# Strassen block sums and one convolution tap moved from VectorE to ScalarE copies and GpSimd's adding DMAs, with a third pair and a new instruction order

## The chip, the cores and the metric

The kernel runs on one core of one Trainium2 chip. The metric is the device time of one execution in microseconds (us). Five engines work beside each other, each through its own instructions in order: TensorE (PE: matrix products into PSUM), VectorE (DVE), ScalarE (ACT), GpSimd (POOL) and SyncE (SP), which here only issues DMAs. An instruction waits for semaphores that other engines or DMAs raise; whatever stands behind it on its engine waits too.

## The reference

Eight batches of 576 tokens go through a packed attention in eight heads and then a gated layer. All is float32.

```python
p_packed = sm_attn(p, k, v)              # 32 packed queries a head attend to k, v
out = sm_attn(q, p_packed, p_packed)     # q attends to the 32 packed rows
x = out.transpose(0, 2, 1, 3).reshape(B, S, H * D)           # [8, 576, 512]
h = np.maximum(x @ w_in, 0.0)                                # [8, 576, 1024]
conv_out = sum(conv_w[k] * hp[:, k:k+S, :] for k in range(3))  # hp: h padded by a zero row at both ends
gate = 1.0 / (1.0 + np.exp(-conv_out))
return h * gate @ w_out                                      # [8, 576, 512]
```

## The kernel before

**Precision.** Every large product is made of three: each operand is split into a rounded high part (hi, made by an ACT copy that rounds) and the rest (lo, a DVE subtraction), and hi·hi, lo·hi and hi·lo are added in PSUM.

**Stages of a batch.** Two groups of four heads a batch (16 groups g) go through `attention`. `packed_weight` folds the packed rows into w_in, and its result is split into `ghi` and `glo`. `ffn1(b, j)` makes 128 of the 1024 hidden columns of batch b (j from 0 to 7): 12 row groups of L705 on PE, then on ACT the relu into one of three `hbuf` buffers (L717) and the middle tap into `hgt` (L721), on DVE the two outer taps (L723, L727), on ACT the tanh (L731) and on DVE the gate (L733). `hgt` has two buffers, for even and odd batches.

**Last product.** The 4608 tokens form 36 tiles of 128 (m). A plain tile takes 24 matmuls of 128x512 columns (L794); its operand is split by ACT and DVE first (L744 and L747, or in two blocks by L850 and L853). Its result is copied by ACT (L858) and stored by SP (L860).

**Pairs.** Two tiles m and m+1 with m in `PAIRS = (29, 32)` are multiplied together by Strassen's scheme in Winograd's form: each is cut into two column blocks (A11, A12 of tile m and A21, A22 of tile m+1), w_out into four quarters, and seven products P of 12 matmuls of 128x256 columns (L926, `products`) stand in for 48 of 128x512. The price is sums: four of token blocks, S1 to S4, a pair (`combined`, one DVE instruction each, L894; S2 needs S1, S4 needs S2), four of weights, T1 to T4, once (`whole_quarter` L966 and `weight_sum` L978, two DVE instructions each), a split of each (L897 and L899; L989 and L991), and two additions a pair in `results` (L951).

**Order.** `ORDER`, a string of two-character numbers, says whose step comes next; there is a stream of steps for each load, group, weight, `ffn1`, tile and sum. `Flow.run` takes them in that order, checks each against a small model of the engines, and emits them; every engine then runs its instructions as they were emitted. The model's constants (`ISSUE`, `LATER`, `SLACK`) alter the emitted program in one way only: where the model sees PE wait before the first tile of the last product, `fill` puts in dummy products of the identity (L251, "idle" in the rows).

**Start.** Loads are issued by SP in order. Up to eight of them fly at once. PE's first product of a later stage is the `packed_weight` of batch 0 (L641), which waits for the loads of groups 0 and 1; its `ghi` and `glo` are needed by the first `ffn1`, and those of its second half by `ffn1(0, 4)`.

Of the kernel before, what the change touches and what calls it, by code (L numbers as in the profile page):

```python
# [26 lines left out]
    "1a0u1n0m0u124f6e1n451l4d4e4f6e0u454f4d1a4h1c4e4e0u0u4f4g1b0y1k4d451b4i4f4f114j4i881n884k4i6e1g4h6f4j6e6e4i6f6e4k"
    "4h4k4i4j4i89161i121a4k4j4i6e1i6f6f121e1a4j4k4l891d126f6f6f6f4j4k4l1i6f1o4k6g121s4l1i4l6g4h124l8a4m1a4l6f1a1j4m1q"
    "191j1i1a6f4m4j121i6g1q8a1w6g6h6e4n6g4m6h1q204n1a1v6g1i6g4m1v4l1h6g4m1a4n124m121r1v4n6g6g236f8b1a6g4o121i4n1i4o4p"
    "6h6h4o4p4p1a236h124o8b4o6h4n1q6g4p1a6h6h6h4p6h4o1m4o1a1y4n234p4p1q1i6h1i1q4q282b1y4r6i1r1y6i1y1a1i6i126i6i1q1a2b"  # L30
    "4r6i12241a4q4q1z6i6j1a6i1a4r1i6i6i4s6i2b1p4s6j4s1q4t4u1q4s1i1y1i4t4s264t1t4t1q1z6k1y2g6j2c4u6j1y4u4s261i6j2j4u6j"
    "4s6k6j264u2j4v4t2j1q6j271i4u1u4v226i4u6j266j4t2e1x4w2k6j4t1i4v1q2e1i1q6k4w2e4v2a1i1q6h2f2e4v3p6k6k6k4w1y1i274x26"
    "6k1q6k6l1y4x6l216k6k6k2f4x1q6k4x2m1y4v50266m1q6l6l4w264v1q26262r2m6l2h4w6l2m2r506l4x2r6j6l4y4w2e1q2n2z4y4y2z1y1y"
    "2z374x1q296l2n2o6l6l6l4w4z4z1y1y4y4z516m4y6m6m6m6m6m1q4y6m6m504z4x4z514z4y524z256n6m526n536m52536n526n1y52535452"
    "536n54546n6n6n6n6n1y1y522w552m2e6o54556o1y266n2s51532u2e2u6n5a54376o6p5553556p1y552654546o3c305a1y6o6o6o6o372e2e"
    "6o6o2p1y6o265656566p6p266p6p532u556q6m26562u576p5556266p6p57566p3f576q56586p59266q6q576q6q58582d5957592m58583457"
    "58596q6q6q596o6q575859596r2e26322m5a6q6r26262e6s5b6r6r6r3226262m2e326s2m2m6r2i6p5b6r2e5c6r6r6q5b6r5c322e5d335c6r"
    "3f3f6s5c6s2v5c2u2e5c2v2e2e2e6s5e6t5c6t355f385d5d5d5d6s6s6s6s2l5f5f5e5e2e6s3a5e5d3a2m6s2m2u2m5k3a5f2m5d2u2q3b2u6t"
    "6u6u6t6r6t6t5f5e5k5f2m5g5f5e6t6t6t5k6t3g6t5h6u6u6u326u5h5h2t6s2m2m6u3a6v5h2m5h5e5h6u6u2x332u6u2m2e5h2y2e5i5j5g5g"
    "6t5i5g2m5i3i5j6v325i5j6u5l3i2u325l325i5j5j3b5g2u362m5i5i2m6v6v6v6v3a2u5j3i5g5j2u5g6v326v6v6v6v6v6w5m5m5l6w313i2u"  # L40
    "2u6x6x5n5n5o6w6w6w6w2u6w2u5n6w6w5o5m6u5m5o6w6w323j3a5m5o5o5n6x6x2u6x6x6y326x6x5n5o5o5m5n3i5m3a3a6x5n5p5p5q5p325q"
    "6x5r3d6y3e396x325p5p5q5q2u5q5p6y6y323a325p5r5r6y6y6y6y6y2u5s2u5q5q5t6y6z6x3j32325r5u325s6w32323a5t6z5r325t3i5s5t"
    "6y5r5v5s5t5s3i6z5s6z3i5r5s6z6z6z6z6z6z5t5u6y5t5u70706z3a3a5w5w703a707071828470705x5w3h5v715w5x70708070705y71715w"
    "83813a3a70715y5w855y5x5x7172835w5y725y5x713i717185715v715z5z72725z5z723a3a723i5z3a5z713i64725x73645y5z727272603i"
    "723i7386605x3i607473733a73723i6z615y607g60643i3i3a60607373733a6162747362627373636174637474747473623i636261636274"
    "3i6563613i63633i656162816175747466676587747466757j7h686666676766757575676867836675767575756766686775757j696a7k7k"
# [1022 lines left out]
```

## Time and profile before

| | |
|---|---|
| median of 3 runs | 403.42 us (401.45 to 403.48) |
| profiled execution, its own time | 402.01 us |
| its span, first to last instruction | 400.2 us |
| PE busy | 392.2 us (98%) |
| DVE busy | 365.5 us (91%) |
| ACT busy | 284.1 us (71%) |
| POOL busy | 1.6 us |
| granted TensorE clock | 0.999 |

1.8 us of the profiled execution lie outside its span. An engine's busy time is the time in which an instruction of it runs. Matmuls are pipelined and their ends are modelled, so how fast PE works is read from the distance between starts, as the chain of waits gives it, and a DVE or ACT instruction's cost to its successor is likewise start to start, some 0.1 us below its duration.

### The profile page before, as it was taken

How to read it: one execution, taken by the hardware profiler on the slowest of the kernel's cores; microseconds unless marked ns; L12 is line 12 of the kernel's file. 1: busy time of each engine (PE TensorE's matmuls, PEld its weight loads, DVE VectorE, ACT ScalarE, POOL GpSimd, SP SyncE). 2: the span in 40 equal slices, each digit the busy share in tenths (PEclk: the TensorE clock that was granted, in tenths of full speed). 3: DMA queues.
4: the chain of work that ended last, by engine and by line, in shares of the span. 5: the costliest groups of instructions: out<-in, count | busy, mean ns of one | idle time of the engine just before them, and what ended most of it. 6: DMA issues, size and time to landing. Idle time of an engine off the chain costs nothing.

```text
span 400.2 us, 8463 instructions
## 1 busy us (share of the span) xinstructions
PE 392.2 (98%) x3393; PEld 318.8 (80%) x3393; DVE 365.5 (91%) x532; ACT 284.1 (71%) x497; POOL 1.6 (0%) x16
## 2 busy tenths in 40 slices
PE   7899999999999999999999999999999999999996
PEld 6668676778868877878869687878788787889996
DVE  0789999999999999999999999999999999999751
ACT  4989999977687588666765659738657678876440
POOL 1000000000000000000000000000000000000000
PEclk9999999999999999999999999999999999999999
DMA  8999999999858782966483539113600110001202
GB/s 304 357 361 267 276 264 163 128 156 146 121 94 112 122 196 68 156 88 153 79 153 79 97 100 157 48 51 97 122 2 27 52 41 19 23 2 52 78 28 79
DMA packets 140378, 49.19 MB, mean 123 GB/s; under 512 B 121244, under 2 KB 132788, under 8 KB 140340
## 3 DMA queue, kind: packets, MB, share of 16 engines
q1 hardware_dynamic: 140340, 48.67, 55.8%
q8 instruction: 26, 0.43, 0.5%
q14 instruction: 12, 0.10, 0.1%
HBM read 37.25 MB, written 9.44 MB: 117 GB/s over the span
## 4 chain that ended last, share of the span: by engine, by line
PE 84%; ACT 8%; DMA 5%; SPq 1%; issue 1%
PE fo L794 44%; PE big L705 23%; PE big L460 3%; PE big L641 3%; DMA q<-in_q_dram 3%; PE big L926 3%; DMA v<-in_v_dram 2%; PE sm L926 2%; PE sm L557 2%; ACT hgt L731 1%; ACT hgt L721 1%; PE big L547 1%; ACT hgt L275 1%; ACT glo L664 1%; SPq L404 1%; PE sm L794 1%
## 5 line engine op out<-in xcount | busy, mean ns | idle before, releaser
L794 PE MATMUL fo<-wo_hi,xhi 128*128 128x512 f32 x240 | 97.9, 408 | 0.0
L794 PE MATMUL fo<-wo_lo,xhi 128*128 128x512 f32 x240 | 94.8, 395 | 0.0
L794 PE MATMUL fo<-wo_hi,xlo 128*128 128x512 f32 x240 | 94.5, 394 | 0.0
L717 ACT ACTIVATE hbuf<-big 128x576 f32<-128x576 f32 x64 | 42.3, 668 | 30.1 <-PE big L705 29.5
L731 ACT ACTIVATE hgt<-hgt 128x576 f32<-128x576 f32 x64 | 43.9, 696 | 18.8 <-DVE hgt L727 18.6
L794 PEld LDWEIGHTS fo<-wo_hi,xhi 128*128 128x128 f32 x240 | 45.3, 189 | 13.3 <-issue 2.5
L705 PE MATMUL big<-a2hi,ghi 128*128 128x288 f32 x256 | 55.6, 298 | 0.1
L705 PE MATMUL big<-a2hi,glo 128*128 128x288 f32 x256 | 54.5, 294 | 0.0
L705 PE MATMUL big<-a2lo,ghi 128*128 128x288 f32 x256 | 54.3, 294 | 0.0
L794 PEld LDWEIGHTS fo<-wo_lo,xhi 128*128 128x128 f32 x240 | 45.1, 188 | 11.2
L723 DVE SCALAR_TENSOR_TENSOR hgt<-hbuf,cw,hgt 128x576 f32<-128x576 f32 x64 | 51.1, 802 | 2.5 <-ACT hgt L721 2.3
L794 PEld LDWEIGHTS fo<-wo_hi,xlo 128*128 128x128 f32 x240 | 45.1, 188 | 7.9
L727 DVE SCALAR_TENSOR_TENSOR hgt<-hbuf,cw,hgt 128x576 f32<-128x576 f32 x64 | 50.7, 803 | 0.4
L721 ACT ACTIVATE hgt<-hbuf,cw 128x576 f32<-128x576 f32 x64 | 50.3, 792 | 1.0
L733 DVE SCALAR_TENSOR_TENSOR hgt<-hgt,hbuf 128x576 f32<-128x576 f32 x64 | 47.1, 745 | 0.7 <-ACT hgt L731 0.4
L705 PEld LDWEIGHTS big<-a2hi,ghi 128*128 128x128 f32 x256 | 42.7, 188 | 5.1 <-ACT glo L664 1.0
L705 PEld LDWEIGHTS big<-a2lo,ghi 128*128 128x128 f32 x256 | 40.9, 188 | 0.0
L705 PEld LDWEIGHTS big<-a2hi,glo 128*128 128x128 f32 x256 | 40.9, 188 | 0.0
L747 DVE TENSOR_TENSOR xlo<-hgt,xhi 128x1024 fp32r<-128x1024 f32 (+1 forms) x36 | 35.8, 1002 | 0.0
L858 ACT COPY o<-fo 128x512 f32<-128x512 f32 (+1 forms) x32 | 18.5, 580 | 21.2 <-PE fo L794 19.6
L744 ACT CAST xhi<-hgt 128x1024 fp32r<-128x1024 f32 (+1 forms) x36 | 31.5, 881 | 2.2 <-DVE hgt L733 2.2
L515 DVE TENSOR_REDUCE nm<-big 128x1 f32<-128x576 f32 x16 | 11.9, 746 | 11.6 <-PE big L460 11.5
(191 smaller groups left out, 604.1 us busy)
## 6 DMA issues: line engine op xcount, KB each, us to landing
out_dram<-o SPq DMA_DIRECT2D x35, 256.0 KB, 3.3
v<-in_v_dram SPq DMA_DIRECT2D x16, 512.0 KB, 5.9
k<-in_k_dram SPq DMA_DIRECT2D x48, 144.0 KB, 4.2
q<-in_q_dram SPq DMA_DIRECT2D x48, 144.0 KB, 4.1
hgt<-in_moe_w_in_dram SPq DMA_DIRECT2D x3, 1024.0 KB, 11.2
hgt<-in_moe_w_out_dram SPq DMA_DIRECT2D x3, 1024.0 KB, 6.6
a1T<-stage SPq DMA_DIRECT2D x96, 20.0 KB, 1.8
hgt<-in_k_dram SPq DMA_DIRECT2D x2, 576.0 KB, 5.1
```

The source lines that it names most:

```text
L705: nc.tensor.matmul(out=t[:, hf, :SH], lhsT=w[:, gg, js], rhs=x[:, hf * SH : (hf + 1) * SH], start=n == 0, stop=n == 3 * NG - 1,)
L717: nc.scalar.activation(out=h[:, 1 : S + 1].rearrange("c (f s) -> c f s", f=2), in_=t[:, :, :SH], func=AF.Relu, scale=0.5)
L721: nc.scalar.activation(out=d, in_=h[:, 1 : S + 1], func=AF.Copy, scale=cw[:, NJ + j : NJ + j + 1])
L723: nc.vector.scalar_tensor_tensor(out=d, in0=h[:, 0:S], scalar=cw[:, j : j + 1], in1=d, op0=ALU.mult, op1=ALU.add)
L727: nc.vector.scalar_tensor_tensor(out=d, in0=h[:, 2 : S + 2], scalar=cw[:, 2 * NJ + j : 2 * NJ + j + 1], in1=d, op0=ALU.mult, op1=ALU.add)
L731: nc.scalar.activation(out=d, in_=d, func=AF.Tanh)
L733: nc.vector.scalar_tensor_tensor(out=d, in0=d, scalar=1.0, in1=h[:, 1 : S + 1], op0=ALU.add, op1=ALU.mult)
L744: nc.scalar.copy(out=hi[:, js, o], in_=src[:, js])
L747: nc.vector.tensor_tensor(out=lo[:, js, o], in0=src[:, js], in1=hi[:, js, o].bitcast(F32), op=ALU.subtract)
L794: nc.tensor.matmul(out=t[:, : fs.stop - fs.start], lhsT=x, rhs=w[:, c, fs], start=c + i == 0, stop=c == NJ - 1 and i == 2)
L858: nc.scalar.copy(out=o[:, fs], in_=sums_of[m, q][:, : fs.stop - fs.start])
L926: nc.tensor.matmul(out=turns[m, bank][:, at : at + 256], lhsT=x[:, c, :], rhs=y[:, c, :], start=first and c + i == 0, stop=c == 3 and i == ...
```

## The change

1. **Sums of blocks.** In `combined` the DVE instruction becomes an ACT copy of one operand into the buffer, with its sign, and a DMA issued by GpSimd that adds the other operand to it in place (`accum_op=ALU.add`). S3 and S4 come out with the opposite sign of before, and so do T3 and T4.
2. **Sums of weights.** `whole_quarter`: ACT copies one part, a DMA adds the other. `weight_sum`: ACT negates (not for T4), a DMA adds.
3. **One tap of the last two batches.** For b = 6 and 7 and j = 0 to 6 the third tap is an ACT copy of the shifted, weighted `hbuf` row into a spare place of `hgt` (the rows of j = 6 and j = 7, not yet in use) and a DMA that adds it to the sum that the first tap has left. The middle tap of j = 6 and of j = 7, which writes those places, waits for the DMAs of all earlier j.
4. **A third pair:** `PAIRS = (27, 29, 32)`. Tiles 27 and 28 were plain ones.
5. **A new `ORDER`,** and new constants of the model: GpSimd's issue 900 for 1050, `LATER` 640 for 620, 800 ns of slack on every DMA behind 60 us, separate DMA times for SP and POOL.

In sum GpSimd issues 14 + 12 + 8 = 34 DMAs where it issued none. DVE loses 14 taps, 8 sums of blocks and 8 of weights. The number of dummy rows goes from 35 to 32.

```diff
-    PAIRS = (29, 32)
+    ADDED = (6, 7)
+    PAIRS = (27, 29, 32)
...
         nc.scalar.activation(out=d, in_=h[:, 1 : S + 1], func=AF.Copy, scale=cw[:, NJ + j : NJ + j + 1])
+        if added:
+            yield Step("ACT", 667, after=[("added", b, j - 2)] if j > 1 else ())
+            u = hgt[b % 2][:, NJ - 1 - j % 2, :]
+            nc.scalar.activation(
+                out=u, in_=h[:, 2 : S + 2], func=AF.Copy, scale=cw[:, 2 * NJ + j : 2 * NJ + j + 1]
+            )
...
-        yield Step("DVE", 729)
-        nc.vector.scalar_tensor_tensor(
-            out=d, in0=h[:, 2 : S + 2], scalar=cw[:, 2 * NJ + j : 2 * NJ + j + 1], in1=d, op0=ALU.mult, op1=ALU.add
-        )
+        if added:
+            yield Step("POOL", 1700, sets=[("added", b, j)])
+            nc.gpsimd.dma_start(out=d, in_=u, accum_op=ALU.add)
+        else:
+            yield Step("DVE", 729)
...
-        yield Step("DVE", 601, after=after, take=["s2"], sets=[("xf", m, key)])
+        yield Step("ACT", 520, after=after, take=["s2"], sets=[("xs", m, key)])
...
-        nc.vector.tensor_tensor(out=full, in0=x, in1=y, op=op)
+        nc.scalar.activation(out=full, in_=x, func=AF.Copy, scale=sign)
+        yield Step("POOL", 1800, sets=[("xf", m, key)])
+        nc.gpsimd.dma_start(out=full, in_=y, accum_op=ALU.add)
...
-        nc.vector.tensor_tensor(out=full, in0=x.bitcast(F32), in1=y.bitcast(F32), op=ALU.add)
+        nc.scalar.copy(out=full, in_=x.bitcast(F32))
+        yield Step("POOL", 3500, sets=[("wf", key)])
+        nc.gpsimd.dma_start(out=full, in_=y.bitcast(F32), accum_op=ALU.add)
...
-        nc.vector.tensor_tensor(out=full, in0=fulls[first], in1=fulls[second], op=ALU.subtract)
+        nc.gpsimd.dma_start(out=full, in_=fulls[other], accum_op=ALU.add)
```

**What the new order moves at the start.** ACT's instructions from the `ghi` of batch 0's second half (ghi_654) to its `glo` (glo_655) and the next relu, before; hgt0 is the buffer of batch 0, L275 prepares a piece of a weight, L342 is a low part of w_out, pm is a query tile of a later group, pb the packed rows of group 2:

```order
L656 CAST ghi_654<-big_643 128x1024
L721 ACTIVATE hgt0_76<-hbuf2_80,cw_72 128x576
L275 ACTIVATE hgt1_77<-hgt1_77 128x1024
L731 ACTIVATE hgt0_76<-hgt0_76 128x576
L342 CAST wo_lo_75<-big_661 128x1024
L484 ACTIVATE pm_671<-p_296 128x128
L731 ACTIVATE hgt0_76<-hgt0_76 128x576
L576 ACTIVATE pb_713<-sm_692,rs_613 128x128
L731 ACTIVATE hgt0_76<-hgt0_76 128x576
L664 CAST glo_655<-big_643 128x1024
```

The same stretch on ACT now (ghi_649, glo_650; L750 is the tanh, L725 the relu, L584 makes pb):

```order
L664 CAST ghi_649<-big_629 128x1024
L283 ACTIVATE hgt1_77<-hgt1_77 128x1024
L750 ACTIVATE hgt0_76<-hgt0_76 128x576
L350 CAST wo_lo_75<-big_678 128x1024
L672 CAST glo_650<-big_629 128x1024
L750 ACTIVATE hgt0_76<-hgt0_76 128x576 x2
L725 ACTIVATE hbuf0_78<-big_720 128x576
L584 ACTIVATE pb_737<-sm_696,rs_666 128x128
```

Two tanh and pb now stand behind that `glo`, and pm and a middle tap no longer stand between the two.

**What it moves at the end.** DVE's sums and splits for the pair at tile 32 before (hgt1 is the buffer of batch 7; the sums write s2, the splits follow):

```order
L894 TENSOR_TENSOR s2_4594<-s2_4539,hgt1_77 128x512
L899 TENSOR_TENSOR xlo_4138<-s2_4539,xhi_4137 128x512
L894 TENSOR_TENSOR s2_4597<-hgt1_77,s2_4594 128x512
L899 TENSOR_TENSOR xlo_4138<-s2_4597,xhi_4137 128x512
L894 TENSOR_TENSOR s2_4617<-hgt1_77 128x512
```

The same sums on ACT now (s2_4560 is S1, s2_4603 S2, s2_4640 S4, s2_4669 S3):

```order
L913 ACTIVATE s2_4603<-s2_4560 128x512
L918 CAST xhi_4062<-s2_4560 128x512
L896 CAST xhi_4062<-hgt1_77 128x512
L869 CAST kq_4172<-hgt1_77 128x512
L877 COPY o_4624<-fo_4490 128x512
L913 ACTIVATE s2_4640<-s2_4603 128x512
L918 CAST kT_4404<-s2_4603 128x512
L913 ACTIVATE s2_4669<-hgt1_77 128x512
```

And POOL's last DMAs, which complete them (L743 is the last tap, s2_4424 and s2_4496 are S4 and S3 of the pair at tile 29):

```order
L743 DMA hgt1_77<-hgt1_77 128x576
L915 DMA s2_4424<-hgt0_76 128x4x128
L915 DMA s2_4496<-hgt0_76 128x4x128
L915 DMA s2_4560<-hgt1_77 128x4x128
L915 DMA s2_4603<-hgt1_77 128x4x128
L915 DMA s2_4640<-hgt1_77 128x4x128
L915 DMA s2_4669<-hgt1_77 128x4x128
```

The copy for S2 reads what S1's DMA has left, and that for S4 what S2's DMA has left, so each waits on ACT for a DMA, with four instructions of other work between the two.

## Rows read from the trace of the kernel before

**Rows 1.** The page's part 1: busy us, share of the span, instructions of each engine.
```profile
PE 392.2 (98%) x3393; PEld 318.8 (80%) x3393; DVE 365.5 (91%) x532; ACT 284.1 (71%) x497; POOL 1.6 (0%) x16
```
**Rows 2.** Stretches: us; busy (instructions) of PE, PEld, DVE, ACT, POOL; PEclk; DMA share; GB/s.
```profile
29.39:49.56 20.17, 19.83 (x254) 14.26 (x254) 19.79 (x31) 19.80 (x35) 0.24 (x2) 1.00 1.03 281
49.56:397.10 347.54, 347.46 (x2848) 284.81 (x2846) 329.57 (x473) 243.11 (x416) 0.00 (x0) 1.00 0.51 96
265.00:390.00 125.00, 125.00 (x835) 107.20 (x834) 115.82 (x158) 83.58 (x136) 0.00 (x0) 1.00 0.15 45
```
**Rows 3.** The chain of waits, late: start us, us, engine, tile, line, instructions merged.
```profile
350.15 5.60 PE fo L794 x24
355.75 3.12 PE big L705 x24
...
367.53 4.23 PE big L926 x36
...
397.14 0.37 ACT o L858
```
**Rows 4.** The chain of waits, from 0 to 75 us.
```profile
15.99 12.05 DMA q<-in_q_dram
...
29.46 1.10 PE big L641 x16
...
30.59 0.02 ACT ghi L656
...
47.89 0.91 ACT glo L664
...
50.16 3.41 PE big L705 x24
```
**Rows 5.** PE's dummy products from 29.39 to 49.56 us: count, busy us, mean ns.
```profile
L251 PE MATMUL idle<-ident 128*128 128x128 f32 x22 | 2.9, 275 | 0.0
```
**Rows 6.** Timeline of ACT: start us, us, engine, line, operation, tiles.
```profile
46.11 0.38 ACT L484 ACTIVATE pm<-p 128x128 f32<-128x128 f32 x1
46.32 0.74 ACT L731 ACTIVATE hgt<-hgt 128x576 f32<-128x576 f32 x1
46.89 0.43 ACT L576 ACTIVATE pb<-sm,rs 128x128 f32<-128x128 f32 x1
47.14 0.75 ACT L731 ACTIVATE hgt<-hgt 128x576 f32<-128x576 f32 x1
47.72 1.08 ACT L664 CAST glo<-big 128x1024 fp32r<-128x1024 f32 x1
```
**Rows 7.** Groups of ACT and of DVE, 265 to 400.2 us: busy us, mean ns.
```profile
L721 ACT ACTIVATE hgt<-hbuf,cw 128x576 f32<-128x576 f32 x21 | 16.1, 776 | 0.4
L731 ACT ACTIVATE hgt<-hgt 128x576 f32<-128x576 f32 x24 | 16.0, 681 | 7.9 <-DVE hgt L727 7.8
L897 ACT CAST kq<-s 128x512 fp32r<-128x512 f32 x3 | 1.9, 623 | 0.6 <-DVE s L894 0.6
L733 DVE SCALAR_TENSOR_TENSOR hgt<-hgt,hbuf 128x576 f32<-128x576 f32 x24 | 17.6, 748 | 0.6 <-ACT hgt L731 0.4
L727 DVE SCALAR_TENSOR_TENSOR hgt<-hbuf,cw,hgt 128x576 f32<-128x576 f32 x22 | 17.4, 804 | 0.2
L966 DVE TENSOR_TENSOR kq<-wo_hi,wo_lo 128x1024 f32<-128x1024 f32 x3 | 3.6, 1217 | 0.0
L894 DVE TENSOR_TENSOR s<-hgt 128x512 f32<-128x512 f32 x4 | 2.7, 683 | 0.0
```
**Rows 8.** DMA issues of 265 to 395 us: issues, KB each, median us to landing.
```profile
out_dram<-o SPq DMA_DIRECT2D x17, 256.0 KB, 2.0
```
**Rows 9.** The page's part 6, DMA issues of the whole execution.
```profile
out_dram<-o SPq DMA_DIRECT2D x35, 256.0 KB, 3.3
v<-in_v_dram SPq DMA_DIRECT2D x16, 512.0 KB, 5.9
...
hgt<-in_k_dram SPq DMA_DIRECT2D x2, 576.0 KB, 5.1
```

More of the change, by code (lines that the diff above doesn't have):

```diff
@@ L27 @@
[L27 to L46, printed above, removed]
@@ L50 @@
+    "857v6d817t7q777v7v7t7t7977757d7x7z817w8281797z75757w817w807a7a8275757c7v7x84827585787x82787883858784868478787880"
+    "858584857d86868383877883787b857b867b7887877b787b7b7b7b7b7b8k7b7b8k7b7b7b7b7b7b"
 )
@@ L81 @@
     }
-    ISSUE = dict(SP=(465, 1100), POOL=(1050, 1000))
-    LATER, LANES = 620, 8
+    ISSUE = dict(SP=(465, 1100), POOL=(900, 1000))
+    LATER, LANES = 640, 8
     SLOW = ((4600, 1.28), (5500, 1.7))
+    ROOMY, SLACK = 60000, 800
     def __init__(self, tokens, warm, busy):
@@ L90, in __init__ @@
         self.free = dict(PE=2500.0, ACT=1900.0, DVE=600.0, SP=580.0, POOL=1350.0)
-        self.data = 2700.0
+        self.data = dict(SP=2700.0, POOL=2700.0)
         self.issued = 0
@@ L149, in transfers @@
             self.issued += step.engine == "SP"
-            slow = next((x for t, x in self.SLOW if self.data < t), 1.0)
-            self.data = max(self.data, at + delay) + step.ns / step.parts * slow
+            slow = next((x for t, x in self.SLOW if self.data["SP"] < t), 1.0)
+            ns = step.ns / step.parts * slow
+            start = max(self.data[step.engine], at + delay)
             if step.engine == "SP":
-                self.flights.append(self.data)
-        return at, self.data
+                landed = self.data["SP"] = start + ns
+                self.flights.append(landed)
+            else:
+                landed = self.data["POOL"] = start + min(max(0.0, self.data["SP"] - start), ns) + ns
+                self.data["SP"] = max(self.data["SP"], start) + ns
+        return at, landed + (self.SLACK if at > self.ROOMY else 0.0)
     def run(self, order):
@@ L719, in ffn1 @@
         )
-        yield Step("ACT", 667)
+        added = b in ADDED and j < NJ - 1
+        yield Step("ACT", 667, after=[("added", b, i) for i in range(j if j == NJ - 1 else NJ - 2)] if b in ADDED and j >= NJ - 2 else ())
         nc.scalar.activation(out=d, in_=h[:, 1 : S + 1], func=AF.Copy, scale=cw[:, NJ + j : NJ + j + 1])
+        if added:
[4 more added lines that the diff above has]
+            )
         yield Step("DVE", 729)
@@ L725, in ffn1 @@
         )
-        yield Step("DVE", 729)
-        nc.vector.scalar_tensor_tensor(
-            out=d, in0=h[:, 2 : S + 2], scalar=cw[:, 2 * NJ + j : 2 * NJ + j + 1], in1=d, op0=ALU.mult, op1=ALU.add
-        )
+        if added:
+            yield Step("POOL", 1700, sets=[("added", b, j)])
+            nc.gpsimd.dma_start(out=d, in_=u, accum_op=ALU.add)
+        else:
+            yield Step("DVE", 729)
+            nc.vector.scalar_tensor_tensor(
+                out=d, in0=h[:, 2 : S + 2], scalar=cw[:, 2 * NJ + j : 2 * NJ + j + 1], in1=d, op0=ALU.mult, op1=ALU.add
+            )
         yield Step("ACT", 573)
@@ L961, in whole_quarter @@
         before = dict(T2="T1", T4="T2").get(key)
-        yield Step("DVE", 1135, after=after + [("wf", before)] * bool(before), take=[tag], sets=[("wf", key)])
+        yield Step("ACT", 905, after=after + [("wf", before)] * bool(before), take=[tag])
         t = wk.tile([128, KQ], F32, name=tag, tag=tag, bufs=1 if tag == "kT" else 3)
@@ L965, in whole_quarter @@
         x, y = quarters(k, n)
-        nc.vector.tensor_tensor(out=full, in0=x.bitcast(F32), in1=y.bitcast(F32), op=ALU.add)
+        nc.scalar.copy(out=full, in_=x.bitcast(F32))
+        yield Step("POOL", 3500, sets=[("wf", key)])
+        nc.gpsimd.dma_start(out=full, in_=y.bitcast(F32), accum_op=ALU.add)
     def weight_sum(key):
-        others, first, second, take, kept = dict(
-            T1=(["wf", "T3"], "T3", "T1", ["v", "v"], [("ws", "T2")]),
-            T3=(["wf", "T2"], "T2", "T3", ["wi"], []),
-            T2=(["ws", "T3"], "T2", "T1", ["ad", "ad"], [("ws", "T4"), ("T", "T1")]),
-            T4=(["ws", "T2"], "T4", "T2", ["wi"], [("T", "T2")]),
+        others, other, take, kept = dict(
+            T1=(["wf", "T3"], "T3", ["v", "v"], [("ws", "T2")]),
+            T3=(["wf", "T2"], "T2", ["wi"], []),
+            T2=(["ws", "T3"], "T1", ["ad", "ad"], [("ws", "T4"), ("T", "T1")]),
+            T4=(["ws", "T2"], "T2", ["wi"], [("T", "T2")]),
         )[key]
         after = [("wf", key), tuple(others)] + [("ws", "T1")] * (key in ("T2", "T3"))
-        yield Step("DVE", 1135, after=after, sets=[("ws", key)])
+        if key != "T4":
+            yield Step("ACT", 905, after=after)
+            nc.scalar.mul(out=fulls[key], in_=fulls[key], mul=-1.0)
+        yield Step("POOL", 3500, after=after, sets=[("ws", key)])
         full = fulls[key]
-        nc.vector.tensor_tensor(out=full, in0=fulls[first], in1=fulls[second], op=ALU.subtract)
+        nc.gpsimd.dma_start(out=full, in_=fulls[other], accum_op=ALU.add)
         yield Step("ACT", 905, take=take)
```

45 lines of the change are left out of this document (32 added, 13 removed).

## The prediction

> **What bounds the kernel now.** I read the page's busy times first, then the stretches, then the chain of waits, then single rows. PE is busy for 98% of the span, DVE for 91% [rows 1]; which of them sets the time the shares do not say. The stretches do: from 49.56 to 397.10 us PE is busy for 347.46 of 347.54 us, DVE for 329.57 and ACT for 243.11 [rows 2]. So from 50 us on PE has no hole, and an engine that is relieved there gives nothing by itself: the time there is the sum of PE's own work. Behind it one copy starts at 397.14 [rows 3], and the last store ends the span at 400.2; that tail stays.
>
> Before 50 us it is otherwise. The chain runs over the load of a q, issued at 15.99 and landed 12.05 us later, then the first `packed_weight` on PE at 29.46, then ACT, which from 30.59 to the `glo` of 47.89 is the chain, and at 50.16 the `ffn1` that needs that `glo` [rows 4]. In 29.39 to 49.56 PE is nominally busy, but 22 of its products are dummies [rows 5].
>
> The sum is made against the profiled execution, 402.01 us, and carried over to the median of 403.42, which lies 1.4 above it; the three runs spread by 2.0, so half a per cent (2.0 us) is about what can be told from no change.
>
> **PE's work.** The third pair removes two plain tiles, 48 matmuls of 512 columns: 2 x 5.60 = 11.20 us [rows 3]. It adds seven products of 12 matmuls; 36 take 4.23 us [rows 3], so seven take 7 x 1.41 = 9.87. Net **-1.3 us**, whole on the bound. Nothing else of PE's work changes but the dummies.
>
> **The start.** What lands by q is the same set of loads in both orders, only permuted, so the first `packed_weight` should stand at 29.5 again; a piece of w_in now goes ahead of a k, which could hold its group back, up to 1 us. From there ACT is the chain. Between `ghi` and `glo` of the second half two tanh (46.32 to 46.89, 47.14 to 47.72), pb (46.89 to 47.14) and pm (46.11 to 46.32) are gone [rows 6]: 0.57 + 0.58 + 0.25 + 0.21 = 1.6 us, by which `glo` and the `ffn1` behind it can come earlier. But three of these four are only put off to right behind it, and ACT has no idle time there, 19.80 of 20.17 us [rows 2]; by the next relu it owes them again. What remains is what PE did in the meantime. Dummy rows between the first `packed_weight` and the start of dense work go from 11 (22 products, [rows 5]) to 8, which at 2.9/11 = 0.26 us each is 0.8 us. I take **-0.5 us**, nearer to nothing than to the bound of 1.6, since the work is deferred and not dropped; the range is -1.6 to +1.0.
>
> **DVE, ACT and the DMAs behind 50 us.** DVE loses 14 taps of 804 ns, 8 sums of 683 and 8 of 1217 [rows 7], start to start about 0.74, 0.60 and 1.14: 10.4 + 4.8 + 9.1 = 24 us, and gets 3 back for the splits and additions of the third pair. Cover: it was not the bound, so worth 0. ACT gets 14 copies like the middle tap of 776 ns, 12 copies of sums and 7 of weights (near the split of 623 ns, and twice it): about 24 us, and 2 for the pair. From 265 to 390 us it was busy for 83.58 of 125 [rows 2]; that becomes some 109, or 87%. It is no bound, but a wait on ACT now has only 13% to be repaid from, and relus (which free PE's PSUM banks) stand behind it.
>
> No row shows an adding DMA. Call D the time from its issue until its successor may start. A store of 256 KB takes 2.0 us in this stretch [rows 8] and 3.3 over all [rows 9]; a load of 576 KB took 5.1 [rows 9]. A tap moves 288 KB and must read two operands, so it lies between; I take 3.3, with 2.0 and 5.1 as bounds. The Trainium skill (DMA: Bandwidth & Descriptors, Anatomy of one DMA) gives 2.0 us fixed plus the bytes at 436 GB/s for a DMA from GpSimd, so for a tap an estimate of 2.7; the sum by it would be the same, and no run here shows it yet.
>
> Who waits for D? Between a tap's ACT copy and its tanh stand eight or more other ACT instructions, 5 us at 0.6, mostly enough. The weights have tens of instructions. The tight place is the last pair (tile 32). Behind the end of the last `ffn1` on PE the order still has 13 x 12 products and 42 matmuls of 512 columns ahead of S4's product: 13 x 1.41 + 42 x 5.60/24 = **28.1 us of cover**. The chain it must cover: relu, queue, middle tap, DVE's two taps, tanh and gate (681, 748, 804 ns and their like, [rows 7]) some 6.5 us. The middle tap of j = 7 waits for the DMA of j = 6, which starts half a us before that `ffn1` ends: D above 2.6 adds its excess. Then S1, S2, S4, each a copy of 0.6 and a D, and the split, 1.4, with the hops between engines about 8 + 4 D in all. At 3.3 that is 21 us. S2's copy also stands on ACT behind the copy of a product that PE ends some 13 us after that `ffn1` (9 x 1.41), which makes it at least 17 + 2 D, 24 at 3.3: 4 to spare. At 5.1 both give 28: just covered. So **0**, and beyond 5 us each us of D costs four. Before, the same three sums cost DVE 0.7 us each.
>
> Sum: -1.3 - 0.5 = **-1.8 us**: 400.2 against the profiled execution, **401.6** against the median.
>
> **The rivals.**
>
> *The adding DMAs are late (slower).* Place: ACT's copies for S2 and S4 of the last pair, behind each other on DMAs. It decides from D = 5 us. A load of 512 KB takes 5.9 [rows 9]; GpSimd has issued no DMA in this kernel, and its issue may add to D. At D = 5.9 to 6.3 the chain is 31.6 to 33.2 against 28.1: 3.5 to 5.1 us of holes on PE; with -1.8, and the ACT waits on taps, some **406**. Against it: the DMA engines are 15% busy there [rows 2], and the 5.9 stems from the crowded start. For it: four Ds in a row with no spare path. A rule of the skill speaks for this rival: by SBUF — State Buffer, Who interferes with whom, a DVE instruction in a two-port mode shuts GpSimd out of the ports through which it writes DMA descriptors, for its whole length. By the same page that holds for copies, casts and tensor_scalar, not for sums of two tensors; DVE's groups here are nearly all sums of two tensors, so I do not raise the chance for it.
>
> *The start gives nothing or takes.* ACT's deferred work is repaid before PE can profit, or the k held back by w_in delays a group. Then the pair alone remains, -1.3, less up to 1 us lost: **402.1 to 403.1**, say 402.6. For it: ACT is full from 30.59 on, and three of four instructions are only moved.
>
> *The start gives all.* PE profits by the whole 1.6 us and the dummies' 0.8: -1.3 - 2.4 = -3.7, **399.7**.
>
> **How the numbers follow.** Forecast 401.6 with 0.52 (its own range, from the runs' spread, 400.3 to 402.9), late DMAs 406 with 0.17, start lost 402.6 with 0.18, start gained 399.7 with 0.13. Faster by over 0.5% is below 401.4, slower above 405.4. Faster: 0.13 and 0.25 of the forecast's 0.52, 0.38. Slower: 0.17. Same: the rest, 0.45. The range leaves out the upper half of the late DMAs and the lower half of the start gained: 399.5 to 405.9.
>
> **What would show it.** Right: PE still without a hole from 50 us, two tiles less and seven products more on it; DVE near 345 us and ACT near 308 busy; first product after the second `glo` 1 to 2 us earlier than 50.16; D of 2.0 to 5.1 in the DMA issues of GpSimd; ACT's waits for DMAs in the last 40 us at most a few us, none passed on to PE. Wrong: PE waiting for L918 or L920 near the end, ACT's tap waits passed on to relus, or `packed_weight` later than 29.5. If PE is without holes and the time still does not fall by 1.2, the price of a product or of the start is wrong.

## The result, and the profile after

The changed kernel takes 405.83 us (median of 5 runs, 405.79 to 407.16), the kernel before 402.6 beside it (five runs; the 403.42 above was the median of the first three); the ratio is 1.0091, with a 95% interval of 1.0063 to 1.0118. The kernel is slower by 0.9%, some 3.7 us (the ratio times 402.6), where I had forecast 1.8 us less. Two executions among the experiments, of 766 and 771 us, are left out of every ratio and median.

The page's part 1 and two lines of its part 6 (DMA issues: count, KB each, median us from issue to landing), which answer to [rows 1, 9]:

```profile
PE 392.4 (97%) x3423; PEld 319.2 (79%) x3423; DVE 345.2 (85%) x509; ACT 307.2 (76%) x537; POOL 38.1 (9%) x50
...
hgt<-hgt POOLq DMA_DIRECT2D x14, 288.0 KB, 3.6
...
s<-hgt POOLq DMA_DIRECT2D x12, 256.0 KB, 4.3
```

The busy times are the forecast ones: DVE 345, ACT 307. An adding DMA takes 3.6 us for a tap and 4.3 for a sum of halves by the median, inside the bounds of 2.0 and 5.1. Stretches of the changed kernel (length; busy time of PE, PEld, DVE, ACT, POOL; granted clock; DMA share; GB/s), which answer to [rows 2], with one stretch added:

```profile
29.39:49.56 20.17, 18.87 (x242) 12.86 (x240) 18.13 (x27) 18.63 (x31) 0.25 (x2) 1.00 0.93 263
...
230.00:256.00 26.00, 24.03 (x260) 17.99 (x259) 25.67 (x41) 19.78 (x32) 3.50 (x3) 1.00 0.78 150
...
265.00:390.00 125.00, 125.00 (x867) 108.51 (x866) 99.28 (x140) 104.96 (x173) 31.58 (x30) 1.00 0.70 120
```

From 265 to 390 us PE has no hole, as forecast. From 230 to 256 it idles for 2 us, in five waits. PE's timeline there (in brackets: idle time ahead, and what ended it):

```profile
237.21 0.32 PE L565 MATMUL sm<-v,a1T 128*32 128x64 f32 x8 [0.33 <-DMA v<-in_v_dram]
...
252.05 0.27 PE L565 MATMUL sm<-v,a1T 128*32 128x64 f32 x2 [0.69 <-DMA a1T<-stage]
252.71 0.27 PE L565 MATMUL sm<-v,a1T 128*32 128x64 f32 x2 [0.39 <-DMA a1T<-stage]
253.22 0.30 PE L565 MATMUL sm<-v,a1T 128*32 128x64 f32 x2 [0.24 <-DMA a1T<-stage]
253.85 0.75 PE L565 MATMUL sm<-v,a1T 128*32 128x64 f32 x34 [0.33 <-DMA a1T<-stage]
```

The first wait is for the v of group 13. The others, 1.65 us together, are those of the attention products of group 14, the hole at 250 us in what follows. These products take the blocks of a1T as SP's 16 small DMAs (L545, one issue each; "the moves") land them, one after the other, so SP is late. SP's queue in that stretch (start, length of the issues together, line, transfer, issues):

```profile
229.87 0.44 SPq L396 DMA_DIRECT2D v<-in_v_dram  x1
230.36 0.66 SPq L400 DMA_DIRECT2D v<-in_v_dram  x1
231.12 6.89 SPq L423 DMA_DIRECT2D q<-in_q_dram  x4
238.05 2.15 SPq L396 DMA_DIRECT2D v<-in_v_dram  x1
240.24 0.64 SPq L400 DMA_DIRECT2D v<-in_v_dram  x1
240.99 11.63 SPq L545 DMA_DIRECT2D a1T<-stage  x16
```

And POOL's in the same stretch:

```profile
229.51 1.42 POOL L989 DMA_DIRECT2D kq<-wo_lo  x1 [189.98 <-DMA a1T<-stage]
239.88 1.28 POOL L989 DMA_DIRECT2D kT<-wo_lo  x1 [8.95 <-ACT pb L584]
```

SP never rests here; it goes from issue to issue. But a q's four issues take 6.89 us and the first issue of the next v 2.15, and at 229.51 GpSimd has put an adding DMA of 512 KB on the way, the first weights' sum, T1. In the kernel before the first of these sums starts at 294.9 us, on DVE. So two suspects share the stretch: the bytes of T1 (theory A), and the new order of SP's queue, with two v, a q and two stores ahead of the moves (theory B). How busy the DMA engines are there (columns as above; the last number but one is their share), in the kernel before (two rows) and in the changed one:

```profile
230.00:240.00 10.00, 10.00 (x53) 8.60 (x53) 9.94 (x14) 5.27 (x8) 0.00 (x0) 1.00 0.34 95
240.00:250.00 10.00, 10.00 (x130) 7.50 (x129) 9.85 (x16) 9.16 (x17) 0.00 (x0) 1.00 1.00 162
...
230.00:240.00 10.00, 9.67 (x125) 7.04 (x124) 9.93 (x17) 9.28 (x15) 1.05 (x2) 1.00 1.20 216
```

The start is the other place. The chain of waits of the changed kernel from the second `glo` on, which answers to [rows 4, 6]:

```profile
47.71 0.91 ACT glo L672
48.62 1.16 ACT hgt L750 x2
49.78 0.58 ACT hbuf L725
50.37 0.26 ACT pb L584
50.62 0.59 ACT qT L458
51.21 0.04 issue
51.26 0.79 PE big L713 x4
```

`glo` comes 0.2 us earlier than before, but PE's `ffn1` starts at 51.26 against 50.16: the two tanh and pb that had been put off now stand behind `glo`, and PE waits for what follows them. How much of this is the order and how much this one execution is seen in the section on the start.

### The profile page after: what moved, and what is told of

It reads as the page before. It is cut to its first block, busy times and chain, and to the rows that moved or that the text cites. A ratio compares the mean times of both kernels' runs of the same rounds, so it can differ in the third digit from the quotient of the medians.

```text
span 404.0 us, 8664 instructions
## 1 busy us (share of the span) xinstructions
PE 392.4 (97%) x3423; PEld 319.2 (79%) x3423; DVE 345.2 (85%) x509; ACT 307.2 (76%) x537; POOL 38.1 (9%) x50
## 4 chain that ended last, share of the span: by engine, by line
PE 78%; DMA 8%; SPq 5%; ACT 4%; DVE 3%; issue 1%; DVEq 0%; ACTq 0%
PE fo L813 37%; PE big L713 21%; PE big L947 4%; DMA hgt<-in_moe_w_in_dram 4%; PE big L468 3%; PE sm L947 3%; DMA hgt<-in_q_dram 3%; PE big L649 3%; SPq L545 3%; PE sm L565 2%; PE big L346 2%; SPq L423 2%; DMA hgt<-in_k_dram 1%; PE big L555 1%; PE sm L813 1%
## 5 line engine op out<-in xcount | busy, mean ns | idle before, releaser
L813 PE MATMUL fo<-wo_hi,xhi 128*128 128x512 f32 (+1 forms) x224 | 90.7, 405 | 0.0
L813 PE MATMUL fo<-wo_lo,xhi 128*128 128x512 f32 (+1 forms) x224 | 88.2, 394 | 0.0
L813 PE MATMUL fo<-wo_hi,xlo 128*128 128x512 f32 (+1 forms) x224 | 87.8, 392 | 0.0
L725 ACT ACTIVATE hbuf<-big 128x576 f32<-128x576 f32 x64 | 42.1, 662 | 20.7 <-PE big L713 20.0
L738 DVE SCALAR_TENSOR_TENSOR hgt<-hbuf,cw,hgt 128x576 f32<-128x576 f32 x64 | 51.2, 806 | 7.2 <-ACT hgt L730 6.9
L750 ACT ACTIVATE hgt<-hgt 128x576 f32<-128x576 f32 x64 | 43.5, 690 | 16.1 <-DVE hgt L746 16.0
L813 PEld LDWEIGHTS fo<-wo_hi,xhi 128*128 128x128 f32 x224 | 42.4, 189 | 12.2 <-ACT o L877 1.7
L813 PEld LDWEIGHTS fo<-wo_lo,xhi 128*128 128x128 f32 x224 | 42.1, 188 | 10.1
L813 PEld LDWEIGHTS fo<-wo_hi,xlo 128*128 128x128 f32 x224 | 42.1, 188 | 7.3
L746 DVE SCALAR_TENSOR_TENSOR hgt<-hbuf,cw,hgt 128x576 f32<-128x576 f32 x50 | 39.9, 806 | 0.3
L766 DVE TENSOR_TENSOR xlo<-hgt,xhi 128x1024 fp32r<-128x1024 f32 (+1 forms) x34 | 33.3, 986 | 3.8 <-ACT xhi L763 3.7
L763 ACT CAST xhi<-hgt 128x1024 fp32r<-128x1024 f32 (+1 forms) x34 | 30.0, 884 | 2.7 <-DVE hgt L752 1.6
L989 POOL DMA_DIRECT2D kq<-wo_lo x3 | 4.1, 1363 | 202.9 <-DMA a1T<-stage 190.0
```

The lines of the kernel that those rows point to most:

```text
L725: nc.scalar.activation(out=h[:, 1 : S + 1].rearrange("c (f s) -> c f s", f=2), in_=t[:, :, :SH], func=AF.Relu, scale=0.5)
L738: nc.vector.scalar_tensor_tensor(out=d, in0=h[:, 0:S], scalar=cw[:, j : j + 1], in1=d, op0=ALU.mult, op1=ALU.add)
L746: nc.vector.scalar_tensor_tensor(out=d, in0=h[:, 2 : S + 2], scalar=cw[:, 2 * NJ + j : 2 * NJ + j + 1], in1=d, op0=ALU.mult, op1=ALU.add)
L750: nc.scalar.activation(out=d, in_=d, func=AF.Tanh)
L763: nc.scalar.copy(out=hi[:, js, o], in_=src[:, js])
L766: nc.vector.tensor_tensor(out=lo[:, js, o], in0=src[:, js], in1=hi[:, js, o].bitcast(F32), op=ALU.subtract)
```

## Experiments: the hole at 250 us

Each kernel was timed beside the kernel before on the same chip. The holes in the expectations are idle time of PE beyond the pitch at which its products follow each other, by my own count; the text goes by the idle time that the profile shows.

**Thin weight DMAs.** The first three of the weights' adding DMAs move 16 of 1024 columns:

```diff
-        nc.gpsimd.dma_start(out=full, in_=y.bitcast(F32), accum_op=ALU.add)
+        if key == "T4":
+            nc.gpsimd.dma_start(out=full, in_=y.bitcast(F32), accum_op=ALU.add)
+        else:
+            nc.gpsimd.dma_start(out=full[:, 0, :16], in_=y.bitcast(F32)[:, 0, :16], accum_op=ALU.add)
```

> The changed kernel with the first three adding DMAs of weights (T1, T3, T2, 512 KB each, issued at 229.5, 239.9 and 254.1) cut to 8 KB each, on the same queue and at the same place; the sums of weights are left out in this way. PE has 2.65 us more of holes in 240 to 260 than the kernel before, all in front of products that wait for SP's moves of attention blocks. Theory A, the bytes of these adding DMAs slow SP's own DMAs (the four issues of a q take 6.89 us from 231.1): the holes go, 403.2. Theory B, SP's queue is simply full there, with two v, a q and two stores ahead of the moves: 405.4 to 405.8, holes stay, the q's issues still above 5 us.

402.48 us, ratio 0.9995 (0.9982 to 1.0009). From 230 to 256 us PE is busy for 26.00 of 26 us, against 24.03 in the changed kernel, and a q's four issues take 4.21 us. Theory A holds, and it is the bytes: the DMAs and their order are the same.

**T1 alone on DVE.** One of the 34 adding DMAs (the text below counts 26 by mistake) is undone:

```diff
-        nc.scalar.copy(out=full, in_=x.bitcast(F32))
+        if key != "T1":
+            nc.scalar.copy(out=full, in_=x.bitcast(F32))
...
+        if key == "T1":
+            nc.vector.tensor_tensor(out=full, in0=x.bitcast(F32), in1=y.bitcast(F32), op=ALU.add)
+        else:
+            nc.gpsimd.dma_start(out=full, in_=y.bitcast(F32), accum_op=ALU.add)
```

> The changed kernel with one of its 26 adding DMAs alone, the first (T1, 512 KB, issued at 229.5), put back as a sum on DVE of about 1.2 us at the same place; ACT's copy for it is gone. With the three weight DMAs thin SP's four issues of the q of group 13 took 4.21 us and the v behind it 0.84, beside the full ones 6.89 and 2.15. Theory A1, the first DMA alone does this: issues near 4.2 and 0.8, holes at 250 below 0.8, 402.5 to 403.2. Theory A2, the second one (T3, at 239.9, beside the moves themselves) has its share: 404 to 405.

402.34 us, 0.9993 (0.9980 to 1.0006). SP's queue of this kernel:

```profile
229.68 4.00 SPq L423 DMA_DIRECT2D q<-in_q_dram  x4
233.72 0.94 SPq L396 DMA_DIRECT2D v<-in_v_dram  x1
234.71 0.64 SPq L400 DMA_DIRECT2D v<-in_v_dram  x1
235.51 12.11 SPq L545 DMA_DIRECT2D a1T<-stage  x16
```

From the start of the q's issues to the first move it is 5.83 us, against 9.87 with T1's DMA beside them. By these 4 us the moves come late, and PE's wait at 250 is gone with them. With T3's DMA issued at 238.35 into them the moves take 12.11 us, 10.98 with thin DMAs, but PE waits for nothing there. A1 holds. The issues also get longer without an adding DMA, when other loads are in flight: in the kernel before a q's four take 2.67 us at 219.88 and 5.18 at 237.94.

**v and q ahead of the moves.** SP's order alone is changed:

```diff
+L396 DMA v_87<-in_v_dram 128x4x256
+L400 DMA v_87<-in_v_dram 64x4x64
+L423 DMA q_2914<-in_q_dram 32x36x32 x4
 L545 DMA a1T_2919<-stage_70 32x160 x16
 L879 DMA out_0_dram<-o_2828 128x512
 L879 DMA out_0_dram<-o_2944 128x512
-L396 DMA v_87<-in_v_dram 128x4x256
-L400 DMA v_87<-in_v_dram 64x4x64
-L423 DMA q_3038<-in_q_dram 32x36x32 x4
 L396 DMA v_88<-in_v_dram 128x4x256
```

> The changed kernel with the loads of v and q of group 13 moved on SP's queue from behind the 16 moves of group 13 to ahead of them, by which the moves of group 14 can start some 3 us earlier; the adding DMAs stay. Theory B, SP's order is the cause: holes at 250 to 254 gone or below 0.5 us, 403.3 to 404. Theory A, the traffic of the adding DMAs: whatever SP issues beside them is slowed, holes stay at 1.5 us or more, 405 to 406.

404.48 us, 1.0045 (1.0019 to 1.0070), with single runs from 402.5 to 407.0. Neither theory had the place: the moves of group 13 (issued from 223.72 to 235.47) now land beside T1's DMA (227.74), and PE waits 1.5 us for them at 234 to 237, then 0.9 us at 238 for a copy of ACT that waits for a store queued behind them. That whatever SP issues beside T1 is late is theory A's mechanism; the time lies between the two ranges. What that does is seen in the stretches of this kernel (columns as above; the third number from the end is the granted clock, of which 1.00 stands for 2.4 GHz):

```profile
230.00:235.00 5.00, 4.63 (x67) 2.90 (x65) 4.93 (x8) 4.29 (x7) 0.00 (x0) 1.00 0.81 126
235.00:240.00 5.00, 3.01 (x44) 2.13 (x44) 1.83 (x6) 2.19 (x4) 0.00 (x0) 0.77 0.68 196
240.00:245.00 5.00, 5.00 (x14) 3.90 (x13) 4.44 (x8) 3.73 (x7) 1.28 (x1) 0.55 0.56 112
```

PE idled 2.4 us in waits of at most 0.9, and the clock was granted at 0.77 in these 5 us and at 0.55 in the next, close to its lower level of 1.2 GHz: 14 products in 5 us where PE is busy throughout. Executions of this kernel at a mean clock of 0.998 or more took 402.5 to 404.5 us, those at 0.991 to 0.996 404.7 to 407.0. So a hole can cost more than its width, and not in every execution. The changed kernel shows the same in small: 405.8 in three executions at 0.996 to 1.00, 406.7 and 407.2 in two at 0.994.

**The weights' sums later.** No instruction is changed. ACT's copies for T1, T3 and T2, their adding DMAs and the splits stand some 19 us later in the order (ACT's rows around T1's copy, later part):

```diff
-L987 COPY kq_3001<-wo_hi_74 128x1024
-L527 ACTIVATE a1_3005,sm1_3006<-big_2830,nm_2932 128x576
+L527 ACTIVATE a1_3003,sm1_3004<-big_2830,nm_2932 128x576
...
 L730 ACTIVATE hgt0_76<-hbuf2_80,cw_72 128x576
 L725 ACTIVATE hbuf1_79<-big_3199 128x576
+L987 COPY kq_3219<-wo_hi_74 128x1024
```

> The changed kernel with all its instructions; only the steps of the first three weights' sums (ACT's copies, the adding DMAs, the splits on ACT) stand about 19 us later in the order, so that the first adding DMA starts near 246 instead of 229.5, when SP has issued q and v and has most moves of group 14 behind it. Theory A, the traffic at that place is the cause and not the DMAs as such: holes at 250 below 0.8 us and 402 to 403. Rival: later they meet the moves and loads of group 15, which wait in their turn, or ACT waits for the adding DMAs: 404 to 406.

**401.38 us, ratio 0.9971 (0.9961 to 0.9981)**: faster than the changed kernel by 4.4 us and than the kernel before (402.53 beside it) by 1.2. POOL's queue and SP's of this kernel:

```profile
246.85 1.43 POOL L989 DMA_DIRECT2D kq<-wo_lo  x1 [208.38 <-DMA a1T<-stage]
250.31 1.28 POOL L989 DMA_DIRECT2D kT<-wo_lo  x1 [2.03 <-ACT kT L987]
...
230.66 4.03 SPq L423 DMA_DIRECT2D q<-in_q_dram  x4
...
236.56 10.95 SPq L545 DMA_DIRECT2D a1T<-stage  x16
```

The moves start 5.90 us after the q again, and between 230 and 400 us PE waits for nothing that the profile shows. So the same bytes, 17 us later, cost PE nothing that the profile shows. With the thin DMAs and T1 on DVE that settles A against B; what remains open is why an issue of SP lasts up to 3 us beside them (the profile shows no wait in it, only a long issue).

## Experiments: the start

**The old loads.** SP's first 26 loads in the order of before (two of the places):

```diff
-L357 DMA s2_129<-in_moe_conv_w_dram 24x256
 L412 DMA hgt0_76<-in_k_dram 128x1152
+L357 DMA s2_130<-in_moe_conv_w_dram 24x256
...
+L412 DMA k_196<-in_k_dram 128x1152
 L313 DMA hgt1_77<-in_moe_w_in_dram 128x2x1024
-L412 DMA k_193<-in_k_dram 128x1152
```

> The changed kernel with SP's first 26 loads put back into the order of the kernel before; nothing else moves. Of the 3.4 us by which the last product comes later, the start up to 60 us holds about 1.4 (PE's holes and dummies 25.97 us there, 24.55 before). Theory 1, the permuted loads cost it: 404.4 us, and the holes of 1.26 and 0.89 us in front of the q transposes at 18.4 and 27.4 are gone. Theory 2, the new order of PE and ACT at the start costs it and the loads do not: 405.8 or more, up to 407, since the engines then meet the loads in an order they were not arranged for.

407.65 us, 1.0130 (1.0092 to 1.0167), above both theories. In this run PE's wait for v at 237 us grew from 0.33 to 0.97, the waits at 252 were as before (1.6), and the clock fell behind them (0.80 in 254 to 256, 0.67 in 256 to 260), so it does not tell the start apart. I repeated it where that hole is gone:

> The kernel with the weights' sums later (401.38), and SP's first 26 loads in the order of the kernel before, as in the run with the old loads. It weighs the start apart from the traffic at 230, which in that run also cost a fall of the clock. My prediction valued the start at -0.5 and named the permuted loads as its risk. Theory 1, the new loads are a loss that the rest hides: 400.5. Theory 2, they suit the new order of PE and ACT: 402 to 403. Theory 3, the loads do not matter: 401.4 within 0.5.

402.74 us, 1.0006 (0.9982 to 1.0029), against 0.9971 with the new loads: theory 2. With the old loads PE waits 1.03 us for a v at 46 us in its profile. The permuted loads were no loss.

How far the start swings by itself is seen at the `ffn1` behind the second `glo`. Eleven kernels here run the same instructions up to there (all but the two with the old loads). In their profiles this `ffn1` starts at 49.26 to 51.26 us, with a median of 49.88; the changed kernel's profile is the latest of them, the kernel with later weights has 50.19, and the one profile of the kernel before has 50.16. The second `glo` starts at 45.60 to 47.59 us by ACT's timeline, with a median of 46.03, against 47.72 before. So the new order does bring `glo` forward, by some 1.7 us, and most of that is lost again between `glo` and `ffn1`: 3.5 us in the chain of the changed kernel (47.71 to 51.26) and 2.3 before (47.89 to 50.16). My first reading of the trace put 1.4 us of the loss on the start; most of that was this swing.

## Experiments: what DVE's relief is worth

**No adding DMA.** All 34 go back to DVE at the same places, ACT's copies are left out (one of the three kinds):

```diff
-            nc.gpsimd.dma_start(out=d, in_=u, accum_op=ALU.add)
+            nc.vector.scalar_tensor_tensor(
+                out=d, in0=h[:, 2 : S + 2], scalar=cw[:, 2 * NJ + j : 2 * NJ + j + 1], in1=d, op0=ALU.mult, op1=ALU.add
+            )
```

> The changed kernel with every sum back on DVE, at the place in the order where GpSimd's DMA stood: the 14 taps, the 12 sums of halves and the 8 sums of weights, ACT's copies for them left out. Third pair and new order stay. My prediction gave DVE's relief the value 0 and the adding DMAs the cost 0: then 405.8, with DVE near 369 us busy, and 403.2 if the bytes of the adding DMAs make the holes at 250. Rival, the relief is what pays for the third pair: DVE late for splits and gates in the last 60 us, 408 or more.

407.60 us, 1.0115 (1.0090 to 1.0140): no hole for a DMA, and yet not faster than the changed kernel, whose interval overlaps this one. The next run shows how much of it the weights' sums do.

**The weights' sums on DVE**, all eight, taps and sums of halves left to DMAs:

```diff
-        nc.gpsimd.dma_start(out=full, in_=y.bitcast(F32), accum_op=ALU.add)
+        nc.vector.tensor_tensor(out=full, in0=x.bitcast(F32), in1=y.bitcast(F32), op=ALU.add)
...
-        nc.gpsimd.dma_start(out=full, in_=fulls[other], accum_op=ALU.add)
+        nc.vector.tensor_tensor(out=full, in0=fulls[other], in1=full, op=ALU.add if key == "T4" else ALU.subtract)
```

> The changed kernel with all eight sums of weights on DVE, as before the change, but at the new places in the order; taps and sums of halves stay adding DMAs. It takes the weights' traffic off and gives DVE back 8 times 1.14 us. If DVE had room for it, as my prediction's value 0 for DVE's relief says: 402.5, as with thin DMAs, or 402 since ACT loses seven copies. Rival: with every sum on DVE there were holes of 0.74 and 1.15 us at 248 and 257 behind ACT and DVE, so the weights' sums do not fit there: 404 to 406.

405.15 us, 1.0065 (1.0052 to 1.0079). PE's waits in this kernel from 230 us on (us in total, times, longest):

```profile
PE big L713 <- DVE s L599: 1.1, 1, 1.1
PE sm L565 <- ACT ppT L592: 0.7, 1, 0.7
PE big L947 <- ACT o L964: 0.7, 1, 0.7
PE fo L813 <- ACT o L877: 0.5, 1, 0.5
```

The first two end at 258.00 and 249.85 us, behind sums that stand on DVE at 252.33 and at 244.05 to 246.37. DVE is busy there, in 230 to 256 us, for 25.67 of 26 us in the changed kernel already, without the sums, so a sum placed there pushes what PE waits for. T1's sum alone did no such harm (402.34). Before, the same sums stood behind 290 us. The rival holds, for these places. The kernel with no adding DMA lies 4.8 us above the kernel before and this one 2.6; what makes the other 2.2 was not taken apart.

**Taps, and sums of halves, on DVE**, each on the kernel with later weights (the diff of the taps is the one above; for the sums of halves `tensor_tensor` takes the DMA's place in the same way):

> The kernel with the weights' sums later (401.38) and the 14 taps back on DVE (10.4 us), ACT's copies for them left out; sums of halves and of weights stay adding DMAs. If DVE's relief is worth nothing from 265 us on, as predicted: 401.4 within 0.5, or a little less since ACT loses 14 copies and the PE's wait for ACT at 357 goes. Rival: the third pair's splits need that time of DVE: 402.5 to 404.

401.53 us, 0.9967 (0.9953 to 0.9982): the taps' relief, 10.4 us of DVE, is worth nothing, with ACT relieved of its 14 copies in turn. The taps' DMAs are not quite free themselves: the profiles with thin DMAs, with T1 or all weights' sums on DVE and with the old loads on later weights show ACT waiting 1.6 to 2.2 us for a tap's DMA near 357 us (at 360.62 in the one with all weights' sums on DVE) and PE waiting 0.3 to 0.7 us for a copy of ACT behind it. With the taps on DVE PE waits for nothing there.

> The kernel with the weights' sums later (401.38) and the 12 sums of halves back on DVE (0.69 us each, 8.3 in all), ACT's copies left out; taps and weights stay adding DMAs. The last pair's chain over S1, S2, S4 has 0.1 us to spare (the split of S4 ends at 386.37, its product starts at 386.49). If only that chain counts, it becomes 10 us shorter and the kernel stays at 401.4 or gains up to 0.3. Rival, DVE has no room for 8.3 us there: 402.5 to 404.

402.29 us, 0.9984 (0.9968 to 1.0000). Its interval overlaps that of the kernel with later weights; it is between its two theories and settles neither. In its profile PE waits once, 0.6 us at 389.62, for a copy of ACT.

## Experiments: the cover in the last pair

**All sums of halves twice,** on the kernel with the thin weight DMAs.

```diff
         nc.gpsimd.dma_start(out=full, in_=y, accum_op=ALU.add)
+        nc.gpsimd.dma_start(out=full, in_=y, accum_op=ALU.add)
```

> The kernel with the three thin weight DMAs (402.48), and behind each of the 12 adding DMAs for the sums of halves a second, equal one on the same tile, which has to wait for the first: D for these sums goes from 4.3 to some 8 us and more; the sums come out wrong in this way. By the prediction's cover of 28.1 us in the last pair the chain of 8 + 4 D is 41 at D = 8.3: holes of some 13 us in the last 40 us, 415. Rival, there is more cover than I counted, since S1 and S2 need not wait for the middle tap of the last gate alone: under 406. Either way the pairs before it may lose some.

443.51 us, 1.1013 (1.0998 to 1.1028): 41 us more, not 13. I had priced the last pair alone, but PE's first wait, 4.1 us, ends at 353.85, ahead of the last pair: all three pairs have such a chain, since S2 needs S1, S4 needs S2 and s2 has two buffers. PE waits some 28 us in all, and at a mean clock of 0.969 its work takes longer too.

**The last pair's twice**, on the kernel with later weights (`if m == PAIRS[-1]:` ahead of the second DMA):

> The kernel with the weights' sums later (401.38) and a second, equal adding DMA behind each of the last pair's four alone, so that D there goes from 4.3 to some 9; its sums come out wrong in this way. Prediction: 8 + 4 D against 28.1, each us beyond D = 5 costs four: 16 us, 417. What the trace of the last pair shows: three D stand in the chain (S1, S2, S4), with 0.1 us to spare at 4.3: 3 times 4.7, 14 us, and something for a lower clock behind the holes: 416 to 420. Rival, cover that neither counts: under 410.

418.71 us, 1.0387 (1.0366 to 1.0409), inside what its trace had given, 416 to 420; the 417 of the prediction's sum is too near for the run to tell the two apart. The last pair's chain in the kernel with later weights, on ACT, POOL, DVE and PE:

```profile
368.22 0.64 ACT L913 ACTIVATE s<-hgt 128x512 f32<-128x512 f32 x1
...
374.59 0.63 ACT L913 ACTIVATE s<-s 128x512 f32<-128x512 f32 x1 [2.18 <-DMA s<-hgt]
...
379.85 0.63 ACT L913 ACTIVATE s<-s 128x512 f32<-128x512 f32 x1 [2.59 <-DMA s<-hgt]
...
385.03 0.62 ACT L918 CAST kq<-s 128x512 fp32r<-128x512 f32 x1 [2.12 <-DMA s<-hgt]
...
369.16 1.29 POOL L915 DMA_DIRECT2D s<-hgt  x1 [4.71 <-ACT kq L869]
375.52 1.28 POOL L915 DMA_DIRECT2D s<-hgt  x1 [5.07 <-ACT s L913]
380.77 1.28 POOL L915 DMA_DIRECT2D s<-hgt  x1 [3.98 <-ACT s L913]
...
385.68 0.69 DVE L920 TENSOR_TENSOR kq<-s,kq 128x512 fp32r<-128x512 f32 x1 [3.37 <-ACT kq L918]
...
386.49 0.40 PE L947 MATMUL sm<-wo_hi,kq 128*128 128x256 f32 x2
```

From each DMA of POOL to the ACT instruction that it releases it is 5.43, 4.33 and 4.26 us (4.67, 4.32 and 4.28 in the changed kernel). The last split ends at 386.37, and S4's product starts at 386.49 on PE without a wait: 0.12 us to spare. The same two rows of the changed kernel leave 1.21 us:

```profile
388.63 0.69 DVE L920 TENSOR_TENSOR kq<-s,kq 128x512 fp32r<-128x512 f32 x1 [3.38 <-ACT kq L918]
...
390.53 0.40 PE L947 MATMUL sm<-wo_hi,kq 128*128 128x256 f32 x2
```

With the last pair's DMAs doubled, PE waits for this chain, and the clock falls behind its holes:

```profile
380.00:390.00 10.00, 6.94 (x26) 5.90 (x27) 2.58 (x4) 2.66 (x5) 2.56 (x2) 0.66 0.60 105
390.00:400.00 10.00, 4.33 (x30) 3.55 (x28) 1.29 (x2) 2.61 (x6) 3.87 (x3) 0.92 0.55 62
400.00:410.00 10.00, 8.57 (x42) 7.42 (x43) 3.36 (x5) 1.96 (x5) 1.28 (x1) 0.74 0.46 71
```

## Why the prediction was wrong

- **The third pair, -1.3 us: right.** In the chain of the changed kernel 36 of the new kind of products take 4.29 us and a plain tile 5.60, which gives -1.2. With the hole out of the way (later weights) the whole kernel stands 1.2 us below the kernel before, 0.8 to 1.6 by its interval; the start, by its median 0.3 us earlier, is too small to tell in that.
- **The start, -0.5 us: not shown either way.** Its argument came out: `glo` moved forward by 1.7 us at the median, and most of it was repaid behind `glo`. What is left is 0.3 us at the median, inside a swing of 2.0 us between executions of the same instructions. The sign that I named, an `ffn1` 1 to 2 us earlier than 50.16, asked for more than my own term.
- **DVE's relief, 0: right for the taps, wrong for the weights' sums**, because they moved to where DVE is full. In their new places the relief from seven of the eight is worth some 2.8 us (405.15 against 402.34 with T1 alone on DVE). For the sums of halves it is open.
- **The adding DMAs, 0: the step that failed.** It asked only who waits for an adding DMA's result ("The weights have tens of instructions"). Nobody waits for that of T1. But I took the DMA share from 265 to 390 us, 15%, where the sums of halves run; T1's DMA is issued at 229.5, beside SP's loads, where the share is 1.20 in 230 to 240 us and 1.03 without it (T1 on DVE). What its bytes do to SP's transfers had no term in the sum: 4 us on SP's queue, 2 us of idle PE, and 3.5 us between the medians (405.83 against 402.34). Not all of the 3.5 need be T1's: in the two profiles 1.4 us of it stand ahead of T1, at the first `ffn1` behind `glo` (51.26 and 49.88), where the programs are still the same. The row that would have warned me was in the trace of the kernel before: its share is 1.00 in 240 to 250 us, where its order has the loads of two q. The Trainium skill states what was missing (DMA: Bandwidth & Descriptors, Issuing engines are not separate DMA queues): DMAs issued from GpSimd and SP run on the same 16 engines and interleave. The runs agree with it: without T1's bytes a q's four issues on SP take 4.00 us, with them 6.89.
- **D and the cover.** D lay in its bounds by the medians, 3.6 and 4.3 us, but not always: the sum of halves issued at 363.71 in the changed kernel landed after 6.0 us, and S1's in the last pair of the kernel with later weights released ACT after 5.43. By the Trainium skill (DMA: Bandwidth & Descriptors, Anatomy of one DMA) a tap was estimated at 2.7; the trace has 0.9 more. The cover was 28.07 us in the changed kernel (last `ffn1` ends at 362.46, S4's product starts at 390.53) and 28.47 with later weights (358.02, 386.49); 28.1 was forecast. The chain took 26.86 and 28.35 us, 1 and 2 more than 17 + 2 D gives at the mean D of its three sums, 4.42 and 4.67. With 1.21 and 0.12 us to spare over three D, late sums decide from a mean D of 4.7 to 4.8 (an estimate), not far below the 5 of the prediction.
- **The late rival's 406 was met by luck.** The measured 405.83 lies beside it and, by 0.07 us, inside my range, whose upper end that rival had set. Its mechanism, PE waiting for the sums of the last pair, is not in the profile of the changed kernel.
- **What would show it.** DVE, ACT and the absence of holes from 265 us on came as written. "PE still without a hole from 50 us" failed at 250. That is where the forecast sign was lost. Waits of ACT for taps, which I had named as a sign of being wrong, are passed on to PE in four profiles of the experiments, by 0.3 to 0.7 us, and not in that of the changed kernel.

## What to carry to other kernels

When work goes from an engine to DMAs, price two things: how long the result takes, and what its bytes do to the transfers already queued at that place, above all to a queue that is full and that PE will wait for some 20 us later. The same DMAs cost some 4 us or nothing, by where they stand in the order; so look up the DMA share at their new place, beside the loads that stand there, and not where most of their kind run. A chain that just fits should be re-timed before it is called covered. And a term of half a microsecond at the start can't be read from one profile, when the same instructions swing by 2 us there.

## What was not expected of the hardware

- One adding DMA of 512 KB from GpSimd, issued 1.6 us ahead of them and landed 8.1 us after its issue, made SP's four issues of a q take 6.89 instead of 4.00 us, and the first issue of the v behind them 2.15 instead of 0.94.
- The start of one and the same row of products swung from 49.26 to 51.26 us over eleven profiles with the same instructions up to there.
- PE holes of 2.4 us went with a granted clock of 0.77 in the same 5 us and 0.55 in the next 5; the same kernel took from 402.5 to 407.0 us, the longer times at the lower mean clock.
- An adding DMA between tiles of SBUF takes 3.6 us for 288 KB and 4.3 for 256 KB in pieces of 512 bytes, by the median from issue to landing in the changed kernel; the eight of 512 KB of weights take 4.5 to 8.1.
